# In the last 256 tokens the copy-out waits for the skip score, and the whole order is planned anew

## The chip, the cores and the metric

The kernel runs on one core of a Trainium2 chip. The metric is the time of one execution in microseconds (us) as the device measures it, as the median of several runs. TensorE (PE) does the matrix products, VectorE (DVE), ScalarE (ACT) and GpSimd (POOL) the elementwise work, and SyncE (SP) issues nearly all transfers.

## The reference, cut to what matters

Three stages follow each other for 4 x 768 = 3072 tokens of 8 heads x 48 = 384 channels: a linear attention with a complex decay, a wide elementwise layer between two matrix products, and a gated mixture of experts that runs only for tokens whose skip score is above zero.

```
S = a_t * S + k_t v_t^T          # complex decay a_t, the real part is read
y_t = q_t S                      # 3072 tokens x 384
h = y @ w_in                     # 384 x 2048
g = (a0 + a1 h + a2 h^2 + a3 h^3) / (1 + |b0||h| + |b1| h^2 + 1e-6)
x = g @ w_out                    # 2048 x 384
skip = x @ w_skip                # one score for each token
out = x, and for tokens with skip > 0 an expert's output is added
```

With the inputs of this case the flags that the kernel works out at its end (is any token's score positive, is any decay out of range) are zero, and the branch to the experts isn't taken: the profile ends with the flags and the closing of the program.

## The kernel before, in words

**Units, chunks and steps.** The tokens are worked in 12 units of 256 tokens (u = 0 to 11), each of two chunks of 128. For a chunk the attention part makes decay sums (`cumx`, `cuml`: matmuls L651 to L681), rotated keys and queries, their transposes (`xp`, L729, onto PE and evicted by `xpe`, L735 on ACT or L737 on DVE), scores (`sc`, L749), their mask (`msk`, L754 on DVE), outputs (`ymm`, L772 and L774), the update of the state (`upd`, L795), and the output's eviction (`yev`, L813 or L814), a transfer inside SBUF (`ysd`) and its rounding (`xhi`, L827). Products L749, L772, L774 and L795 use PE in column tiles of 64 ("column-tiled" below); all others use the whole array.

For a unit the wide layer has 8 steps (p = 0 to 7). A step has two halves of G1 (L886, into a `zb` bank, 9 matmuls each), the elementwise chain (ACT L866 and L387, DVE L870), the split of its result in a rounded part `gh` (L915) and a remainder `gl` (L918), and two G2 (L938, 6 matmuls each, accumulated over the 8 steps into `ob[0]` and `ob[1]`, one for each half of the tokens). Unit 0 does G1 and G2 with unsplit float32 weights, because splitting the weights (`whi` L480, `wlo` L485) is done while it runs; later units use a three-product split.

**At the end of a unit** `ob[t]` is copied with a scale into `x2` (`ev`: L387 on ACT or L951 on DVE), sent to the output (`st`), and read once more by DVE for the skip score (`sk`, L956). The first G2 of the next unit may write `ob[t]` when both have read it. Before, `sk` names `x2` among what it reads, so it always follows the copy.

**What sets the order.** A planner, `Plan.order`, runs on the host: it has a cost for each task, a latency for each hop, ranks with an offset for each kind of task and unit (the table `PP`), and picks for each engine the next task. The result is written out as a fixed order for each engine; there is no choice left on the chip. Where the planner sees PE without work ahead of `start(NP) + X1`, `filled` puts dummy matmuls there (L1025, L1029 and, after the first 48, L1032): they keep PE running, and since they stand in PE's order, they take their time on the chip whether PE is idle or not.

**The end of the program.** After the last `sk`, `flags` (L1329 to L1338) sums the flags, PE adds them over the partitions (L1335), and all engines load the result, branch, and close.

Of the kernel before, what the change touches and what calls it, by code (L numbers as in the profile page):

```python
# [29 lines left out]
class Plan:  # L30
# [36 lines left out]
    def order(self, slack, bias, ahead, hold, cold, only):  # L67
# [22 lines left out]
        def finish(t, end, e):  # L90
            for s in t.succ:
                wait[s.n] -= 1
                lat = self.LAT[e] if e else 0.0
                if len(s.opts) == 1 and s.opts[0][0] == e and e != "SP":
                    lat = 0.06
                ready_at[s.n] = max(ready_at[s.n], end + lat)
                if wait[s.n] == 0:
                    if s.only and s.only[0].eng != s.only[1]:
                        done[s.n] = True
                        finish(s, ready_at[s.n], None)  # L100
                    else:
                        heapq.heappush(events, (release(s), 1, s.n, None))
# [78 lines left out]
    def filled(self, out, first, last, gap, each, fn):  # L181
# [6 lines left out]
                end = max(end, at + cost)  # L188
            fns.append((at, len(fns), f))
        return [f for _, _, f in sorted(fns, key=lambda x: x[:2])]  # L190
PP = dict(RK={('e1', 3): -0.0, ('qr', 1): 6.96, ('d3', 3): 13.1, ('sk', 3): -33.76, ('msk', 1): -5.9, ('e6', 3): -0.19, ('cumx', 1): -2.3, ('xhi', 2): 6.15, ('e5', 3): 0.49, ('G2', 1): -4.22, ('a5', 2): 2.01, ('a2', 1): -8.56, ('dec', 1): -3.76, ('kr', 1): -14.26, ('lda', 0): 5.23, ('e4', 3): 21.04, ('ev', 3): -14.56, ('prr2', 2): 5.78, ('consts2', 0): -4.33, ('tlo', 3): -1.17, ('e8', 2): 8.49, ('ev', 0): -21.56, ('consts', 0): -6.3, ('a5', 3): 1.52, ('upd', 1): 11.25, ('e7f', 2): -15.18, ('prr1', 1): -3.2, ('G1', 2): -3.49, ('xlo', 2): -3.85, ('ldk', 2): 15.32, ('G2', 2): 13.59, ('d4', 1): -1.28, ('xp', 2): -0.57, ('S2', 2): -13.35, ('alo', 2): 6.39, ('e7f', 3): 4.78, ('yev', 1): -13.54, ('prr1', 3): 0.46, ('tlo', 2): 16.11, ('dec', 3): 8.54, ('e9', 3): 4.88, ('ysd', 1): -1.18, ('e1', 1): -4.49, ('last', 3): -1.04, ('cry', 3): 0.22, ('a2', 0): 5.36, ('S2', 1): 7.88, ('xabs', 0): 14.95, ('upd', 3): 1.28, ('cadd', 1): -16.46, ('e11', 2): -3.49, ('qr', 3): -3.75, ('ldq', 0): 31.15, ('a4', 2): 2.25, ('red', 2): -8.46, ('rnd', 2): 3.88, ('lnexp', 0): -3.85, ('wldi', 0): 0.65, ('e9', 2): 19.04, ('G1', 3): -3.79, ('e2', 1): 2.32, ('lda', 1): 6.73, ('ldv', 1): 2.97, ('exq', 1): 2.55, ('thi', 3): -1.29, ('a2', 3): 1.22, ('kr', 2): 11.48, ('a4', 0): -4.77, ('e2', 3): -0.12, ('S', 1): 1.63, ('ev', 1): 40.5, ('e6', 1): -7.3, ('d1', 3): -1.59, ('e11', 1): 1.23, ('rnd', 3): 25.29, ('e3', 1): 3.94, ('sc', 2): 4.01, ('e9', 1): -5.69, ('a4', 1): -1.23, ('e13', 0): 20.66, ('last', 0): 4.52, ('sc', 1): -6.19, ('cry', 1): -8.01, ('wb3', 0): -0.35, ('clear', 0): -0.5, ('upd', 0): -1.87, ('ysd', 2): -2.76, ('e4', 1): -2.8, ('st', 1): -33.79, ('e3', 2): 9.5, ('kr', 3): 1.89, ('gl', 2): -3.18, ('xpe', 2): 1.47, ('e8', 1): 0.91, ('e7', 3): -0.07, ('xp', 3): -0.38, ('cuml', 2): 8.38, ('a5', 0): -0.18, ('sk', 1): -8.68, ('e8', 3): -2.46, ('sk', 0): 0.63, ('ldk', 3): 0.52, ('xabs', 3): 3.07, ('e11', 3): 7.67, ('a1', 2): -0.63, ('xhi', 0): 19.42, ('prr2', 3): 0.27, ('d2', 3): -4.57, ('wb2', 0): 0.47, ('S', 0): 5.86, ('e1', 2): 28.44, ('rnd', 1): 5.16, ('last', 1): -9.33, ('prr1', 0): 18.07, ('e7', 2): -0.5, ('yev', 3): -1.48, ('e8', 0): 0.22, ('msk', 2): -4.38, ('exq', 2): -4.69, ('ldc', 0): 8.32, ('st', 3): -5.42, ('ysd', 0): -16.93, ('exp', 2): 14.54, ('qr', 0): 7.46, ('upd', 2): 0.53, ('S2', 0): 22.86, ('trig', 0): -0.15, ('lda', 2): -11.3, ('st', 2): -4.62, ('cf', 0): -11.69, ('xlo', 1): 0.91, ('xp', 0): 1.47, ('cuml', 0): 0.35, ('xp', 1): 0.1, ('e10', 1): 10.75, ('e2', 2): 1.32, ('ldv', 3): -1.82, ('exp', 0): 1.38, ('d1', 2): 0.8, ('last', 2): -3.81, ('cuml', 1): 4.83, ('e10', 2): 18.95, ('ysd', 3): 5.28, ('xlo', 3): 1.57, ('ymm', 1): -2.42, ('exp', 3): 5.64, ('exq', 0): 4.26, ('whi', 0): 0.0, ('gl', 3): 1.62, ('exp', 1): 0.28, ('dec', 2): -0.18, ('ldv', 2): 0.29, ('e5', 1): -0.67, ('e5', 0): -0.28, ('qr', 2): -5.24, ('red', 1): 0.08, ('ahi', 2): -0.51, ('e6', 2): -11.75, ('gh', 3): -0.5, ('exq', 3): 2.27, ('xpe', 0): -1.55, ('cumx', 2): -2.59, ('st', 0): 13.52, ('e6', 0): 5.22, ('cry', 2): -0.66, ('ymm', 0): 1.91, ('S', 3): 0.34, ('e7f', 1): 3.39, ('ldk', 0): 1.33, ('e3', 0): -8.95, ('xhi', 1): 5.57, ('sk', 2): 3.32, ('G2', 3): -0.73, ('d4', 3): 1.65, ('ldq', 2): 12.25}, FU=1, C2=5.371, C3=117.794, AF=1.733, P0=3.406, P1=8.248, NO={'whi': ('POOL',), 'prr2': ('POOL',), 'prr1': ('POOL',), 'gh': ('ACT', 'DVE'), 'cadd': ('DVE',), 'wlo': ('DVE',), 'tlo': ('DVE',)}, E0=8.284, E1=-3.522, TC=16, WS=(0, 1, 2, 3, 4, 5, 0, 1, 1, 0, 1, 2, 2, 1, 2, 2), HO={('tlo', 'POOL'): 0.482, ('tlo', 'DVE'): 0.437, ('gl', 'POOL'): 0.129, ('cadd', 'DVE'): 0.404, ('xpe', 'DVE'): 0.549, ('prr1', 'DVE'): 0.413, ('last', 'POOL'): 0.369, ('ev', 'DVE'): 0.055, ('xabs', 'DVE'): 0.192, ('xhi', 'DVE'): 0.444, ('prr1', 'POOL'): 0.11, ('xlo', 'DVE'): 0.101, ('whi', 'ACT'): 0.177, ('gh', 'DVE'): 0.558, ('prr2', 'POOL'): 0.087, ('gh', 'ACT'): 0.067, ('last', 'ACT'): 0.097}, DW=54.14194888235853, WL=7, P=6.353, LAG2=4.235, SL={'ACT': 2.875, 'DVE': 0.975, 'POOL': 0.839, 'SP': 0.306, 'PE': 1.002, '2': 2.13}, X1=34.585, T0=55.875, NZ=6, NH=3, CU=2, BI={'DVE': 67.612, 'POOL': -2.285})


def main_part(tc, ctx, q, k, v, a_re, a_im, w_in, w_out, moe_a, moe_b, w_skip, out, keep):
# [661 lines left out]
    def step(s):  # L856
# [88 lines left out]
        if p == NP - 1:  # L945
            for t in range(2):
                o, x = ob[t][:, 0:DM], x2[t]
                ti = 2 * u + t
                X2 = ("x2", t)
                pl.add([act(0.47, x, o, AF.Copy, scale=fine["sg"]),  # L950
                        ("DVE", 0.53, lambda x=x, o=o: nc.vector.tensor_scalar(  # L951
                            out=x, in0=o, scalar1=fine["sg"], scalar2=None, op0=ALU.mult))],
                       reads=[("o", t), "cf"], writes=[X2], name="ev", due=at(1, 3))
                pl.add(dma((out[ti * 128:(ti + 1) * 128, :], x)), reads=[X2], writes=[("out", ti)], name="st", due=at(1, 5))
                sk_ = ("zk", ti)
                pl.add([("DVE", 0.65, lambda o=o, ti=ti, sk_=sk_: nc.vector.scalar_tensor_tensor(  # L956
                    out=zb[pl.slot[sk_]][:, 0:DM], in0=o, scalar=fine["sg"], in1=wsk, op0=ALU.mult, op1=ALU.mult,
                    accum_out=skip[:, ti:ti + 1]))],
                       reads=["wsk", "cf", ("o", t), X2], bank=sk_, free=sk_, name="sk", due=at(1, 3))
# [477 lines left out]
```

## Time and profile before

| | |
|---|---|
| time, median of 3 runs | 647.55 us (646.91 to 648.62) |
| the profiled execution's own time | 647.43 us |
| its span, first to last instruction | 645.7 us |
| PE busy | 633.9 us, 98% of the span |
| DVE busy, ACT busy, POOL busy | 558.0, 558.7, 332.2 us |
| dummy matmuls L1032 in the profile | 270 records, two for each of 135 instructions |

The sum in the prediction is made against the profiled execution: 1.7 us of its 647.43 lie outside the span. A matmul's end in the profile is modelled, so matmuls overlap in the rows; the distance from one start to the next tells what one costs.

### The profile page before, as it was taken

The numbers are of one execution on the slowest core, as the hardware profiler recorded it, in microseconds if no ns is written. First come the engines' busy times: TensorE is split into PE (matmuls) and PEld (weight loads), VectorE is DVE, ScalarE is ACT, GpSimd is POOL, SyncE is SP. The second block draws the span as 40 slices with busy tenths as digits, with TensorE's granted clock in tenths as the row PEclk, the third lists the DMA queues.
The fourth block names the chain that finished last, engine by engine and source line by source line (L and its number), as shares of the span: only waits on it lengthen the run. The fifth ranks groups of instructions, "written<-read, shape, count | busy, mean of one in ns | idle before, by whom it ended". The sixth has DMA issues, their size and how long they took to land.

```text
span 645.7 us, 14813 instructions
## 1 busy us (share of the span) xinstructions
PE 633.9 (98%) x5720; PEld 590.3 (91%) x5720; DVE 558.0 (86%) x901; ACT 558.7 (87%) x925; POOL 332.2 (51%) x349
## 2 busy tenths in 40 slices
PE   9999999999999999999999999999999999999994
PEld 8888887789999989999999999999999999989994
DVE  6999999898889987897988989998978997876873
ACT  5889989997899997897999998997998997976771
POOL 5145269397636447547367366545557554522221
PEclk9999999999999999999999999999999999999998
DMA  8955114010401303103112203103112200000000
GB/s 316 401 187 169 50 35 157 16 34 21 123 3 44 99 26 115 39 14 115 30 44 59 78 14 91 52 29 97 53 37 67 68 17 23 19 29 5 19 6 32
DMA packets 29777, 45.79 MB, mean 71 GB/s; under 512 B 5760, under 2 KB 23552, under 8 KB 29696
## 3 DMA queue, kind: packets, MB, share of 16 engines
q1 hardware_dynamic: 29408, 44.73, 21.3%
q8 instruction: 47, 0.77, 0.5%
q14 instruction: 34, 0.28, 0.2%
q10 hardware_dynamic: 288, 0.00, 0.0%
HBM read 38.73 MB, written 4.72 MB: 67 GB/s over the span
## 4 chain that ended last, share of the span: by engine, by line
PE 81%; ACT 12%; DVE 4%; issue 2%; POOL 0%; DVEq 0%; ACTq 0%; POOLq 0%
PE zb L886 27%; PE ob L938 25%; PE zb L729 6%; PE zb L749 5%; PE ob L1032 4%; PE zb L772 4%; PE zb L795 3%; PE zb L774 3%; ACT wk L387 2%; ACT wk L866 2%; ACT tb L548 1%; DVE wk L870 1%; PE zb L678 1%; ACT L584 1%; ACT zb L866 1%
## 5 line engine op out<-in xcount | busy, mean ns | idle before, releaser
L870 DVE SCALAR_TENSOR_TENSOR wk<-wk,cf,zb 128x512 f32<-128x512 f32 x192 | 141.7, 742 | 33.0 <-ACT zb L866 26.3
L886 PE MATMUL zb<-xh,wi 128*128 128x256 f32 x528 | 152.4, 289 | 0.0
L886 PE MATMUL zb<-xl,wi 128*128 128x256 f32 x528 | 147.9, 280 | 0.0
L886 PE MATMUL zb<-xh,li 128*128 128x256 f32 x528 | 147.8, 280 | 0.0
L387 ACT ACTIVATE wk<-wk,cf 128x512 f32<-128x512 f32 x192 | 139.8, 732 | 1.4
L915 POOL TENSOR_SCALAR gh<-wk 128x512 fp32r<-128x512 f32 x88 | 61.4, 698 | 147.3 <-PE ob L938 69.4
L938 PE MATMUL ob<-wo,gh 128*128 128x384 f32 x352 | 120.4, 342 | 0.8 <-DVE zb L956 0.8
L938 PE MATMUL ob<-wo,gl 128*128 128x384 f32 x352 | 118.6, 337 | 0.0
L938 PE MATMUL ob<-lo,gh 128*128 128x384 f32 x352 | 118.2, 336 | 0.0
L918 POOL TENSOR_TENSOR gl<-wk,gh 128x512 fp32r<-128x512 f32 x69 | 99.2, 1438 | 5.3
L886 PEld LDWEIGHTS zb<-xh,wi 128*128 128x128 f32 x528 | 99.5, 188 | 2.7 <-issue 1.0
L886 PEld LDWEIGHTS zb<-xl,wi 128*128 128x128 f32 x528 | 99.7, 189 | 0.6
L886 PEld LDWEIGHTS zb<-xh,li 128*128 128x128 f32 x528 | 99.4, 188 | 0.0
L866 ACT ACTIVATE wk<-zb 128x512 f32<-128x512 f32 x96 | 57.4, 598 | 31.1 <-PE zb L886 30.6
L870 DVE SCALAR_TENSOR_TENSOR zb<-wk,cf,zb 128x512 f32<-128x512 f32 x96 | 71.7, 748 | 0.0
L938 PEld LDWEIGHTS ob<-wo,gh 128*128 128x128 f32 x352 | 66.1, 188 | 2.7 <-issue 2.4
L870 DVE SCALAR_TENSOR_TENSOR wk<-wk,zb 128x512 f32<-128x512 f32 x96 | 65.5, 683 | 1.6
L866 ACT ACTIVATE wk<-zb,cf 128x512 f32<-128x512 f32 x96 | 66.4, 691 | 0.1
L938 PEld LDWEIGHTS ob<-wo,gl 128*128 128x128 f32 x352 | 66.1, 188 | 0.1
L938 PEld LDWEIGHTS ob<-lo,gh 128*128 128x128 f32 x352 | 66.2, 188 | 0.0
L866 ACT ACTIVATE zb<-wk 128x512 f32<-128x512 f32 x96 | 58.2, 608 | 7.7 <-DVE wk L870 7.0
L749 PEld LDWEIGHTS zb<-qT,kT 112*64 112x64 f32 x768 | 35.4, 137 | 5.9 <-ACT qT L735 3.1
(166 smaller groups left out, 1326.9 us busy)
## 6 DMA issues: line engine op xcount, KB each, us to landing
vb<-in_v_dram SPq DMA_DIRECT2D x24, 288.0 KB, 3.0
ws<-in_moe_w_in_dram SPq DMA_DIRECT2D x8, 768.0 KB
ws<-in_moe_w_out_dram SPq DMA_DIRECT2D x8, 768.0 KB, 8.9
kraw<-in_k_dram SPq DMA_DIRECT2D x12, 384.0 KB, 3.8
qraw<-in_q_dram SPq DMA_DIRECT2D x12, 384.0 KB, 3.8
out_dram<-x2b SPq DMA_DIRECT2D x24, 192.0 KB, 1.9
ar<-in_a_re_dram SPq DMA_DIRECT2D x11, 384.0 KB
ai<-in_a_im_dram SPq DMA_DIRECT2D x11, 384.0 KB, 5.7
```

The costliest lines, as they stand in the source:

```text
L387: return ("ACT", cost, lambda: nc.scalar.activation(out=out, in_=in_, func=func, **kw))
L729: nc.tensor.transpose(z[0:112, i, :], src[:, 112 * h:112 * h + 112], ident)
L749: nc.tensor.matmul(z[o:o + 64, h, n:128], lhsT=K[:, h, n:n + 64], rhs=Q[:, h, n:128], start=True, stop=True)
L772: nc.tensor.matmul(dst, lhsT=vt, rhs=pT[hf][:, i, :], start=True, stop=first)
L774: nc.tensor.matmul(dst, lhsT=state[:, 48 * h:48 * h + 64], rhs=qT[hf][:, i, :], start=False, stop=True)
L866: return ("ACT", cost, lambda: nc.scalar.activation(out=h() if out is None else out, in_=h() if in_ is None else in_, func=func, **kw))
L870: return ("DVE", cost, lambda: nc.vector.scalar_tensor_tensor(out=h() if out is None else out, in0=in0, scalar=scalar, in1=h(), op0=op0, o ...
L886: nc.tensor.matmul(h()[:, i * 256:i * 256 + 256], lhsT=w[:, 128 * j:128 * j + 128], rhs=x[:, j, :], start=(n == 0), stop=(n == 3 * len(pr) ...
L915: nc.gpsimd.tensor_scalar(out=g, in0=uu, scalar1=1.0, scalar2=1.0, op0=ALU.mult, op1=ALU.mult)
L918: eng[e].tensor_tensor(out=ghl("gl", s), in0=uu, in1=ghl("gh", s).bitcast(F32), op=ALU.subtract)
L938: nc.tensor.matmul(o, lhsT=a[:, sl], rhs=w, start=(f == 0 and n == 0), stop=(f == NF - 1 and n == len(pr) - 1))
L1032: nc.tensor.matmul(ob[0][:, 384:512], lhsT=ident, rhs=ident, start=n == 32, stop=True, skip_group_check=True)
```

## The change

In the last unit `sk` no longer reads `x2` but `ob[t]` alone, and `ev` follows `sk`. The rounding of the weights (`whi`) gets a third option, on DVE. The planner's latency between two tasks of one engine goes from 0.06 to 0.12 us, and the table `PP` (some 200 numbers, of which a line would tell nothing) is another one; it bars `whi` from DVE and POOL (`NO={'whi': ('DVE', 'POOL'), ...`), and moves the dummies' window and the due times.

```
                 if len(s.opts) == 1 and s.opts[0][0] == e and e != "SP":
-                    lat = 0.06
+                    lat = 0.12
...
+            elif e == "DVE":
+                nc.vector.tensor_scalar(out=hi, in0=weight_f(m, p), scalar1=1.0, scalar2=None, op0=ALU.mult)
...
-        pl.add([("ACT", 0.73, lambda: whi("ACT")), ("POOL", 0.85, lambda: whi("POOL"))], ...
+        pl.add([("ACT", 0.73, lambda: whi("ACT")), ("POOL", 0.85, lambda: whi("POOL")), ("DVE", 0.47, lambda: whi("DVE"), True)], ...
...
-                       reads=[("o", t), "cf"], writes=[X2], name="ev", due=at(1, 3))
+                           reads=[("o", t), "cf"] + ([("sk", t)] if u == NU - 1 else []), writes=[X2], name="ev", due=at(1, 3))
...
-                       reads=["wsk", "cf", ("o", t), X2], bank=sk_, free=sk_, name="sk", due=at(1, 3))
+                           reads=["wsk", "cf", ("o", t)] + ([] if u == NU - 1 else [X2]), writes=[("sk", t)], bank=sk_, free=sk_, name="sk", due=at(1, 3))
...
+                for f in (score, evict) if u == NU - 1 else (evict, score):
+                    f()
```

**In the built program.** Nearly every row on every engine stands elsewhere. The work on PE is the same matmuls, but for the dummies L1032 (L1040 after the change): 135 before, 129 now. Between full-array work, PE's order has 78 runs of column-tiled matmuls before and 84 now. `whi` is 16 instructions on ACT in both, and none on DVE. Of the tasks with a choice of engine, 8 `xpe` move from DVE to ACT (96 on ACT now), 13 `gl` from POOL to DVE (32 now), 6 `xlo`, 4 `qr` and 5 of the scalings L465 to POOL, 6 `cadd` from POOL to DVE.

Three places are shown. The first is PE's order in the program's first tenth, from the state update of the second chunk (L795, L797 after) or the decay sums (L681, L683 after) to the first G1 of unit 0 (L886, L888 after, on `fi`, the unsplit weights). Before:

```order
L795 MATMUL zb_83<-vb_96,kt_107 64x48 x16
L1032 MATMUL ob_77<-ident 128x128 x2
L681 MATMUL zb_79<-ta_154,trir 128x384
L681 MATMUL zb_82<-ta_154,trir 128x384
L1032 MATMUL ob_77<-ident 128x128 x6
L654 MATMUL zb_83<-ai_142,trit 128x384
L1032 MATMUL ob_77<-ident 128x128 x7
L886 MATMUL zb_83<-xh_4_614,fi_297 128x256 x6
```

And now:

```order
L776 MATMUL zb_79<-qT_109,state 64x128 x2
L683 MATMUL zb_82<-ta_153,trir 128x384
L683 MATMUL zb_84<-ta_153,trir 128x384
L797 MATMUL zb_79<-vb_96,kt_107 64x48 x16
L1040 MATMUL ob_77<-ident 128x128 x11
L888 MATMUL zb_81<-xh_4_620,fi_300 128x256 x3
L656 MATMUL zb_79<-ai_142,trit 128x384
```

Between the second chunk's outputs and the first G1 stand 11 dummies in place of 15, and the sum L654 (L656 now) has moved behind the first matmuls of G1.

The second place is PE at the end of unit 5. `ob_77` and `ob_78` are the two accumulators; nine matmuls of G1 stand just ahead of these rows and, ahead of them, the last G2 of unit 5 on `ob_77`. Before:

```order
L938 MATMUL ob_78<-wo_1387,gh_1404 128x384
L938 MATMUL ob_78<-lo_1547,gh_1404 128x384
L938 MATMUL ob_78<-wo_1387,gl_1442 128x384
L938 MATMUL ob_78<-wo_1387,gh_1404 128x384
L938 MATMUL ob_78<-lo_1547,gh_1404 128x384
L938 MATMUL ob_78<-wo_1387,gl_1442 128x384
L938 MATMUL ob_77<-wo_1060,gh_1404 128x384
```

And now, with three groups of transposes between the nine of G1 and the first row:

```order
L940 MATMUL ob_78<-wo_1423,gh_1378 128x384
L940 MATMUL ob_78<-lo_1562,gh_1378 128x384
L940 MATMUL ob_78<-wo_1423,gl_1427 128x384
L940 MATMUL ob_78<-wo_1423,gh_1378 128x384
L940 MATMUL ob_78<-lo_1562,gh_1378 128x384
L940 MATMUL ob_78<-wo_1423,gl_1427 128x384
L731 MATMUL zb_82<-ident,qt_105 112x128 x4
L751 MATMUL zb_83<-qT_108,kT_110 64x128 x2
L751 MATMUL zb_83<-qT_108,kT_110 64x64 x2
L751 MATMUL zb_83<-qT_108,kT_110 64x128 x2
L751 MATMUL zb_83<-qT_108,kT_110 64x64 x2
L940 MATMUL ob_77<-wo_1079,gh_1378 128x384
```

The first G2 of unit 6 on `ob_77` has moved back behind four groups of transposes and one of scores.

The third place is the end of ACT's and DVE's order. The order is the same, and what the rows wait for is not (in brackets, the semaphores of the engines). ACT before, with the copies L387 of `ob` and the load of the flags:

```order
L387 ACTIVATE wk<-wk,cf 128x512 [waits Activation_49] x2
L866 ACTIVATE zb_81<-wk 128x512 [waits DVE_49,Activation_49]
L387 ACTIVATE x2b<-ob_77,cf 128x384 [waits DMAHW4_49,PE_49]
L387 ACTIVATE x2b<-ob_78,cf 128x384 [waits DMAHW5_49,PE_49]
L1364 TENSOR_LOAD fazi [waits DVE_49]
```

And DVE now, with the scores L961 (L956 before), whose waits were for `Activation_49`:

```order
L920 TENSOR_TENSOR gl_1427<-wk,gh_1378 128x512 [waits PE_49,Pool_49]
L961 SCALAR_TENSOR_TENSOR zb_84,skip<-ob_77,cf,wsk 128x384 [waits PE_49]
L961 SCALAR_TENSOR_TENSOR zb_81,skip<-ob_78,cf,wsk 128x384 [waits PE_49]
L1337 TENSOR_SCALAR fat_7024,fam<-skip 128x24 [waits DVE_49]
L1345 CAST fazi<-faz 1x2 [waits PE_49]
```

The scores now wait for PE alone, and ACT's two copies wait for DVE in place of PE.

## Rows read from the trace of the kernel before

**Rows 1.** The page: busy time, share of the span and instructions of each engine.
```profile
PE 633.9 (98%) x5720; PEld 590.3 (91%) x5720; DVE 558.0 (86%) x901; ACT 558.7 (87%) x925; POOL 332.2 (51%) x349
```

**Rows 2.** Busy time of each engine by stretch: us, PE, PEld, DVE, ACT, POOL, PEclk.
```profile
20.00:40.00 20.00, 19.97 (x213) 18.17 (x212) 19.87 (x38) 17.10 (x26) 7.06 (x7) 1.00 0.91 337
340.00:360.00 20.00, 20.00 (x160) 19.62 (x157) 17.75 (x28) 17.75 (x33) 13.67 (x14) 1.00 0.29 82
```

**Rows 3.** Chain of waits at the start (start, us, what), and the dummies' group.
```profile
21.30 1.36 PE zb L681 x4
22.66 5.36 PE ob L1032 x48
L1032 PE MATMUL ob<-ident 128*128 128x128 f32 x270 | 33.0, 276 | 0.0
```

**Rows 4.** Chain of waits: G1 and G2 undisturbed, G1 after L795, scores after either.
```profile
167.00 1.06 PE zb L886 x9
168.06 2.08 PE ob L938 x12
...
363.50 1.27 PE zb L886 x9
...
426.46 1.49 PE zb L749 x32
...
435.41 1.35 PE zb L749 x32
```

**Rows 5.** PE's waits: for whom, total us, times, longest.
```profile
PE ob L938 <- DVE zb L956: 0.8, 2, 0.5
PE zb L886 <- ACT xh L827: 0.3, 1, 0.3
```

**Rows 6.** Timeline of PE and DVE at the end of unit 5.
```profile
370.70 0.34 PE L938 MATMUL ob<-wo,gl 128*128 128x384 f32 x1
371.27 0.41 PE L938 MATMUL ob<-wo,gh 128*128 128x384 f32 x1 [0.23 <-DVE zb L956]
...
370.44 0.62 DVE L956 SCALAR_TENSOR_TENSOR zb<-ob,cf,wsk 128x384 f32<-128x384 f32 x1
370.98 0.14 DVE L956 DVE_READ_ACCUMULATOR zb<-ob,cf,wsk 128x1 f32 x1
```

**Rows 7.** Timeline of PE at a wait for an eviction.
```profile
329.26 0.34 PE L938 MATMUL ob<-wo,gl 128*128 128x384 f32 x1
329.76 0.65 PE L729 MATMUL zb<-ident,qt 128*112 128x128 f32 x4 [0.16 <-ACT kT L735]
```

**Rows 8.** Chain at the start, then ACT's timeline there.
```profile
48.48 0.92 PE zb L795 x32
...
55.20 2.86 PE zb L886 x12
...
48.58 0.60 ACT L813 ACTIVATE ys<-zb 128x512 f32<-128x512 f32 x1
...
53.02 0.84 ACT L480 ACTIVATE wi<-fi 128x768 fp32r<-128x768 f32 x1
53.77 0.56 ACT L664 ACTIVATE cs<-zb,magic 128x384 f32<-128x384 f32 x1
...
54.65 0.51 ACT L827 ACTIVATE xh<-ys 128x384 f32<-128x384 f32 x1
```

**Rows 9.** Timeline of the program's end.
```profile
636.51 0.34 PE L938 MATMUL ob<-wo,gl 128*128 128x384 f32 x1
636.89 0.58 ACT L387 ACTIVATE x2b<-ob,cf 128x384 f32<-128x384 f32 x1 [0.46 <-PE ob L938]
...
637.51 0.63 DVE L956 SCALAR_TENSOR_TENSOR zb<-ob,cf,wsk 128x384 f32<-128x384 f32 x1 [0.36 <-ACT x2b L387]
```

**Rows 10.** DVE's group for one weight operation; the copy-out's transfer to landing (us).
```profile
L458 DVE TENSOR_SCALAR zb<-ws 128x384 int32<-128x384 int32 x32 | 17.1, 554 | 0.1
out_dram<-x2b SPq DMA_DIRECT2D x24, 192.0 KB, 1.9
```

More of the change, by code (lines that the diff above doesn't have):

```diff
@@ L485, in wlo @@
             eng[e].tensor_tensor(out=weight_lo(m, p), in0=weight_f(m, p), in1=weight_hi(m, p).bitcast(F32), op=ALU.subtract)
-        pl.add([("ACT", 0.73, lambda: whi("ACT")), ("POOL", 0.85, lambda: whi("POOL"))], reads=w, writes=h_ + [("st", (p + (NP if m == "o" else 0)) // 2)], name="whi")
+        pl.add([("ACT", 0.73, lambda: whi("ACT")), ("POOL", 0.85, lambda: whi("POOL")), ("DVE", 0.47, lambda: whi("DVE"), True)], reads=w, writes=h_ + [("st", (p + (NP if m == "o" else 0)) // 2)], name="whi")
         pl.add([("POOL", 1.85, lambda: wlo("POOL")), ("DVE", 0.87, lambda: wlo("DVE"), True)],
@@ L949, in step, with evict, score @@
                 X2 = ("x2", t)
-                pl.add([act(0.47, x, o, AF.Copy, scale=fine["sg"]),
-                        ("DVE", 0.53, lambda x=x, o=o: nc.vector.tensor_scalar(
-                            out=x, in0=o, scalar1=fine["sg"], scalar2=None, op0=ALU.mult))],
-                       reads=[("o", t), "cf"], writes=[X2], name="ev", due=at(1, 3))
[L954 to L958, printed above, removed]
-                       reads=["wsk", "cf", ("o", t), X2], bank=sk_, free=sk_, name="sk", due=at(1, 3))
+                def evict(o=o, x=x, ti=ti, X2=X2, t=t):
+                    pl.add([act(0.47, x, o, AF.Copy, scale=fine["sg"]),
+                            ("DVE", 0.53, lambda x=x, o=o: nc.vector.tensor_scalar(
+                                out=x, in0=o, scalar1=fine["sg"], scalar2=None, op0=ALU.mult))],
+                           reads=[("o", t), "cf"] + ([("sk", t)] if u == NU - 1 else []), writes=[X2], name="ev", due=at(1, 3))
+                    pl.add(dma((out[ti * 128:(ti + 1) * 128, :], x)), reads=[X2], writes=[("out", ti)], name="st", due=at(1, 5))
+                def score(o=o, ti=ti, X2=X2, t=t):
+                    sk_ = ("zk", ti)
+                    pl.add([("DVE", 0.65, lambda o=o, ti=ti, sk_=sk_: nc.vector.scalar_tensor_tensor(
+                        out=zb[pl.slot[sk_]][:, 0:DM], in0=o, scalar=fine["sg"], in1=wsk, op0=ALU.mult, op1=ALU.mult,
+                        accum_out=skip[:, ti:ti + 1]))],
+                           reads=["wsk", "cf", ("o", t)] + ([] if u == NU - 1 else [X2]), writes=[("sk", t)], bank=sk_, free=sk_, name="sk", due=at(1, 3))
+                for f in (score, evict) if u == NU - 1 else (evict, score):
+                    f()
     NC = NT // 128
```

2 lines of the change are left out of this document (1 added, 1 removed).

## The prediction

> **What bounds the kernel now.** I read the page first. PE is busy in 98% of the span, DVE and ACT in 86 and 87% [rows 1]: the end of PE's work, and the short tail behind it, set the time. The page alone can mislead here, since PE's share contains the dummies. They are 270 records of L1032, and 48 of them in a row take 5.36 us, so 0.112 us a record and 0.223 us for an instruction of two [rows 3]; 135 instructions are 30 us, all in the first tenth of the program.
>
> Next the busy time by stretch: from 20 to 40 us DVE is the full engine (19.87 of 20 us), while PE looks full because of the dummies; from 340 to 360 PE is full with real work and DVE and ACT have 2.2 us to spare in 20 [rows 2]. The granted clock is 1.00, the higher level of 2.4 GHz, in both stretches; I see no cost of the clock in the sum.
>
> So the time is PE's list of work, plus what PE loses, plus the tail. A busy PE hides small losses, because modelled ends overlap. I therefore looked at starts: G1's nine matmuls take 1.06 us undisturbed, twelve of G2 2.08 us, so 0.118 and 0.173 us from start to start [rows 4]. Where a start comes later and the instruction has a wait, that is a loss. I found eleven such places between 55 and 476 us, of 0.15 to 0.71 us, 3.3 us together. PE's own waits show only a part of it: 0.8 us in two waits for the skip score, 0.3 us for the rounded attention output [rows 5]. One of the two shows the pattern: G2 starts at 370.70 and the next one, into the other accumulator, at 371.27 in place of 370.87, because DVE read that accumulator for the score until 371.12 [rows 6]: 0.39 us lost by the regular pitch (0.57 less 0.17 to 0.18). Another: a transpose starts at 329.76, where the G2 matmul ahead of it started at 329.26, because it waits for ACT's eviction [rows 7]: some 0.33 us.
>
> **The change part by part.** *The weights' rounding on DVE.* The built order has it 16 times on ACT and never on DVE, as before: the new option costs and gives nothing. What it would relieve, ACT at the start, keeps its load.
>
> *The tail.* Before: the last matmul starts at 636.51, ACT copies from 636.89 for 0.58 us, DVE scores from 637.51, and the flags follow it [rows 9]. Now DVE scores where ACT began, at about 636.89, and all behind it moves up by 637.51 - 636.89 = 0.62 us. What is late next is the copy: it starts at about 637.6 (0.63 of the score and a hop of 0.03 to 0.1), ends by 638.2, and its transfer, 1.9 us from issue to landing in the middle [rows 10], lands by some 640.5. The span ends at 645.7, so it is covered as long as the closing behind the flags stays longer than that; SP issues it at about 638.2 for a third of a us and comes to the flags' load at about 638.5, when the flags are ready too. I take -0.62; bounds 0 (SP or the landing sets the end) and -0.65.
>
> *The dummies.* Six fewer: -6 x 0.223 = -1.34 us [rows 3]. This counts in full only if the work behind is ready; where it isn't, PE waits instead, which I count among the losses.
>
> *Runs of column-tiled work.* 84 in place of 78. G1 right behind one takes 1.27 us in place of 1.06: 0.21 us to leave [rows 4]. Two blocks of scores take 1.49 us behind full-array work and 1.35 behind other column-tiled work: 0.14 to enter. So 0.35 a run, 6 x 0.35 = +2.1 us. Beside transposes I found the way out dearer and the way in cheaper; the new runs stand partly among them and among dummies, so the bounds are 1.6 and 2.8. The Trainium skill, page "TensorEngine Tiling (Array Packing)", section "Key Properties", says that a change of the tiling mode drains TensorE, which speaks against this change; the 0.35 us agrees in kind. By that rule alone each added run costs something and the sum of this part would be positive; it gives no size, so the sum goes by the rows.
>
> *Losses that go.* At the end of each unit PE must not come back to `ob[t]` before copy and score are done. In PE's list I summed the work that stands between the last G2 of a unit and the first of the next on the same accumulator, by the pitches above. Before: 2.11 us in four of the 22 places; two of these are the two waits. Now one has 2.11 (end of unit 1), all others 3.1 to 12.8. Likewise from a unit's transposes to its first scores: before, 10 places have under 1.5 us; now two, both in the first 85 us. From scores to the masked product 12 places had under 2 us, now four. So nearly all the 3.3 us should go: -3.3 with bounds 0 and -3.3.
>
> *Losses that come.* At the start the first G1 needs the rounded output of the second chunk. Before, from the start of the state update behind that chunk's product (48.48) to G1 (55.20) are 6.7 us, the last 0.49 of them lost; ACT evicts at 48.58 and is done with the rounding at 55.16 [rows 8]. Now PE has, in between, two decay sums (1.36 us [rows 3]), the update (0.92), 11 dummies (2.45): 4.7 us. ACT has two operations less in that stretch, a rounding of weights (0.75 us from its start at 53.02 to the next) and a rounding of phases (about 0.44, as two operations fill 53.77 to 54.65 [rows 8]), so its 6.6 us become some 5.4: 0.7 us lost. The one place with 2.11 us at an accumulator may lose 0.4 again, and the two or three short returns at the start 0.4. Together +1.5, with bounds 0.3 and 4: what a table with other offsets does at places that I didn't sum can't be read from before.
>
> *Moved between engines.* DVE gets 13 remainders and 6 carries and gives off 8 evictions, 6 remainders of the attention output and 4 products; ACT gets the evictions and gives off 5 scalings. By their rows' durations that is within 5 us for each over 646, where both have some 90 us idle: nothing on the path, except by queueing at the start, which is in the bound of 4.
>
> **The sum.** -0.62 - 1.34 + 2.1 - 3.3 + 1.5 = -1.7 us, from 647.43 to 645.7 us for an execution (span 644.0). The median before, 647.55, lies 0.1 above the profiled execution, so that is -0.3% against it. About 0.3%, 1.9 us, is what a measurement of this kernel can tell from no change: the forecast stands just inside.
>
> **The rivals.** *All waits go.* If the new table leaves only 0.3 us of losses: -0.62 - 1.34 + 2.1 - 3.0 = -2.9, 644.5 us; with the cheaper column runs 644.0. For it: every distance that I summed grew, at accumulators by a factor of 1.5 to 6. Against: the start, where DVE has no slack and G1 is asked for earlier.
>
> *Losses only change place.* The eleven go and as many others come, 3 to 4 us at places with other partners (queueing on ACT, which now does all evictions of transposes): -0.62 - 1.34 + 2.1 + 0 to 1 = +0.1 to +1.1, 647.5 to 648.6 us. For it: before, the order was planned in the same way and still lost 3.3 us, and the wait of rows 7 is behind ACT's queue, not behind a short distance alone.
>
> *The start runs dry, slower.* PE's place in the list asks for unit 0's weights and attention before DVE delivers them. One block of weights is six DVE operations of 0.55 us [rows 10], some 2.8 us at their pitch; two blocks ordered ahead of what PE waits for would cost 5.6 us. DVE has only 0.13 us idle from 20 to 40 us [rows 2], so nothing takes that back. -0.62 - 1.34 + 2.1 - 3.3 + 0.8 + 5.6 = +3.2, 650.6 us. It decides from some 4.3 us of such waits on. Against it: I summed DVE's work ahead of PE's places in both orders, and until 125 us DVE stands as far ahead now as before, within 1 us at the tightest places.
>
> *The tail gives nothing*, since the closing hangs on something else: 646.3 us, inside the forecast's own range.
>
> **How the numbers follow.** Forecast (losses between 0.6 and 2.6 us, time 644.8 to 646.8): 0.55. All waits go, 644.0 to 644.8: 0.17. Losses only change place, 646.8 to 649.4: 0.18. Slower start, 649.5 to 651: 0.10. The range 644.2 to 649.2 leaves out the slow rival and a piece of the fast one. Faster by over 0.3% (under 645.6): all of the second case and four tenths of the first, 0.39. Slower (over 649.5): 0.10. Within: 0.51.
>
> **What would show it.** In the new profile: (1) the score starts within 0.1 us of the last matmul's modelled end and the stretch from that matmul to the end is 0.6 us shorter; (2) 258 records of L1040; (3) G1 behind column-tiled work still 1.27, and 84 such runs; (4) PE's waits for the score at the ends of units gone, at most one left; (5) the first G1 waits for the rounded output, some 0.7 us, at about 54. The prediction is wrong if PE's first 125 us show waits of over 2 us, if later starts behind waits sum to over 3 us, or if PE's own pitch differs between the two.

## The result, and the profile after

The changed kernel takes 655.32 us (median, 654.56 to 655.53), the kernel before in the same comparison 648.01 (646.91 to 648.87): ratio 1.0111, 95% interval 1.0098 to 1.0124, some 7.3 us slower. The forecast was 645.7 with a range of 644.2 to 649.2, so it was wrong, in sign too. The profiled execution has a span of 653.9 us, 8.2 more than before.

First the lines of the page, TensorE's waits and the dummies' group after the change, which answer to [rows 1], [rows 5] and [rows 3].

```profile
PE 636.7 (97%) x5708; PEld 592.1 (91%) x5708; DVE 562.7 (86%) x901; ACT 555.4 (85%) x923; POOL 321.6 (49%) x345
```
```profile
PE zb L731 <- DVE kt L390: 4.2, 1, 4.2
...
PE faz L1343 <- ACT x2b L387: 1.4, 1, 1.4
```
```profile
L1040 PE MATMUL ob<-ident 128*128 128x128 f32 x258 | 34.0, 284 | 0.0
```

The waits for the skip score are gone, as forecast, and one long wait is new, of 4.2 us (beside two of 0.6 and 0.3): the transposes L731 of unit 2's first rotated key wait for DVE. The busy times by stretch around it (us, PE, PEld, DVE, ACT, POOL, granted clock, then transfers):

```profile
120.00:122.00 2.00, 2.00 (x19) 2.00 (x18) 1.93 (x4) 1.99 (x3) 1.92 (x3) 1.00 0.00 0
122.00:124.00 2.00, 0.29 (x3) 0.10 (x1) 1.93 (x3) 1.04 (x2) 1.92 (x2) 1.00 0.00 0
124.00:126.00 2.00, 0.00 (x0) 0.00 (x0) 2.00 (x2) 0.00 (x0) 1.57 (x1) 0.91 0.00 0
126.00:128.00 2.00, 1.49 (x7) 1.49 (x8) 2.00 (x4) 0.35 (x1) 0.00 (x0) 0.50 0.00 0
...
130.00:132.00 2.00, 2.00 (x11) 2.00 (x11) 0.67 (x1) 1.17 (x3) 0.00 (x0) 0.50 0.00 0
132.00:134.00 2.00, 2.00 (x22) 1.53 (x21) 0.55 (x2) 1.82 (x4) 0.00 (x0) 0.89 0.00 0
```

PE stands idle from 122.3 to 126.5. Within that wait the granted clock falls (0.91 in the stretch from 124 to 126), and it is 0.50, the lower level of 1.2 GHz, until about 132.5: the transposes and the dummies among them run at half speed. DVE is full all the while. What it does there, with its timeline and then GpSimd's (start, duration, engine):

```profile
118.37 0.65 DVE L344 TENSOR_SCALAR cf<-cf 128x2 int32<-128x2 int32 x1
119.05 0.48 DVE L365 TENSOR_SCALAR rsum<-cf 128x2 f32<-128x2 f32 x1
119.56 0.46 DVE L344 TENSOR_SCALAR cf<-cf 128x2 int32<-128x2 int32 x1
120.06 1.76 DVE L367 TENSOR_TENSOR cf<-cf 128x1 f32<-128x1 f32 x1
121.75 0.14 DVE L344 TENSOR_SCALAR cf<-cf 128x1 int32<-128x1 int32 x1
121.92 1.79 DVE L369 TENSOR_SCALAR cf<-cf 128x2 f32<-128x2 f32 x1
123.75 0.17 DVE L370 RECIPROCAL cf<-cf 128x2 f32<-128x2 f32 x1
123.95 1.64 DVE L371 TENSOR_TENSOR rsum<-cf 128x2 f32<-128x2 f32 x1
125.51 0.94 DVE L390 TENSOR_TENSOR kt<-r,cs 128x768 f32<-128x768 f32 x1
```
```profile
119.97 1.84 POOL L487 TENSOR_TENSOR li<-fi,wi 128x768 fp32r<-128x768 f32 x1
121.89 1.80 POOL L487 TENSOR_TENSOR lo<-fo,wo 128x768 fp32r<-128x768 f32 x1
123.77 1.80 POOL L487 TENSOR_TENSOR li<-fi,wi 128x768 fp32r<-128x768 f32 x1
```

Eight operations on one or two columns take 7.2 us (118.37 to 125.59). The long ones end where a weight remainder on GpSimd ends: 121.82 and 121.81, 123.71 and 123.69, 125.59 and 125.57. Before, the same eight stood at 75.63 to 77.05, 0.15 to 0.17 us each, in a gap of GpSimd's:

```profile
76.48 0.17 DVE L369 TENSOR_SCALAR cf<-cf 128x2 f32<-128x2 f32 x1
```
```profile
77.71 0.57 POOL L610 TENSOR_SCALAR cs<-cs 1x384 f32<-1x384 f32 x1 [5.96 <-DMA cs<-xr]
```

They are one task of the planner, the last part of `coefs2`, whose results only the flags need. Its price there is 1.3 us, plus once the rest of what GpSimd is doing; in the new order it was put at 119.48 for 1.98 us. The prediction did not look at it.

The program's end after the change, which answers to [rows 9]:

```profile
643.12 0.34 PE L940 MATMUL ob<-wo,gl 128*128 128x384 f32 x1
643.50 0.63 DVE L961 SCALAR_TENSOR_TENSOR zb<-ob,cf,wsk 128x384 f32<-128x384 f32 x1 [0.38 <-PE ob L940]
644.22 0.18 DVE L1337 TENSOR_SCALAR_CACHE_REDUCE fat<-skip 128x24 f32<-128x24 f32 x1
644.22 0.58 ACT L387 ACTIVATE x2b<-ob,cf 128x384 f32<-128x384 f32 x1 [0.48 <-DVE zb L961]
644.85 0.19 PE L1343 MATMUL faz<-fam,one 128*1 128x2 f32 x2 [1.39 <-ACT x2b L387]
645.08 0.15 DVE L1345 CAST fazi<-faz 1x2 int32<-1x2 f32 x1 [0.67 <-PE faz L1343]
```

The last matmul starts at 643.12, 6.6 us later than before [rows 9]. The other 1.6 us of the span lie at its very end: TensorE's last semaphore comes 1.64 us behind SyncE's, before 0.01 behind it; VectorE's last comes with SyncE's in either kernel. The table, from the records of the semaphores, has it for all kernels of this study. "List" is the time from the first decay sum of TensorE's list (L654, L656 after) to the last matmul; that sum starts at 14.9 to 16.2 us, from one execution to the next (13.6 and 14.3 in the two kernels with fewer dummies ahead of it).

| kernel | TensorE records | list, us | last matmul at | SyncE's last semaphore behind it | TensorE's |
|---|---|---|---|---|---|
| before | 5720 | 620.88 | 636.51 | 9.13 | 9.14 |
| after | 5708 | 627.39 | 643.12 | 9.13 | 10.77 |
| e1_cf_late | 5708 | 620.14 | 635.60 | 9.02 | 10.58 |
| e2_dry_recip | 5708 | 620.42 | 636.13 | 9.09 | 11.16 |
| e3_filled | 5746 | 624.96 | 639.86 | 9.02 | 9.03 |
| e4_before_cf_busy | 5720 | 628.87 | 644.04 | 9.04 | 9.05 |
| e5_fewer_dummies | 5680 | 619.84 | 636.02 | 9.41 | 9.42 |
| e6_flag_bank | 5708 | 620.20 | 635.51 | 9.09 | 10.58 |
| e7_tail_undone | 5708 | 620.79 | 636.57 | 9.02 | 10.51 |
| e8_dry_forms | 5708 | 624.88 | 639.93 | 9.22 | 10.72 |
| e9_early_dummies | 5696 | 620.77 | 634.37 | 9.61 | 9.62 |
| e10_less_at_61 | 5668 | 619.89 | 635.30 | 9.46 | 9.48 |
| e11_trimmed | 5656 | 621.63 | 635.96 | 9.21 | 9.22 |
| e12_same_count | 5708 | 620.16 | 636.18 | 9.15 | 10.44 |

Each row of the table is one execution. Four kernels that differ little in what they do up to the last matmul (e1, e2, e6, e7) have lists from 620.14 to 620.79, so a difference under 0.65 us between two rows tells nothing. One of the twelve executions of e12_same_count ran at a mean clock of 0.751 and took 779.96 us; its time and ratio below are those of the other eleven.

The rows of DMA queue q8, which the page calls "instruction", tell more of the closing. Where TensorE's last semaphore is late, it stands 1.34 to 1.62 us behind the end of that queue's last packet of 16 KB (after the change 10.77 and 9.24 us behind the last matmul, in e1 10.57 and 9.10). Where it isn't late, it keeps no such distance (-0.30 to +1.12). At the branch, in all fourteen kernels, TensorE's first record stands 1.35 to 1.62 us behind the end of a packet of 16 KB. So a late closing fits a wait of TensorE for its own last instructions; that it is one, no run shows.

### The profile page after: what moved, and what is told of

It is laid out like the page before. It is cut to its first block, busy times and chain, and to the rows that moved or that the text cites. A ratio compares the mean times of both kernels' runs of the same rounds, so it can differ in the third digit from the quotient of the medians.

```text
span 653.9 us, 14722 instructions
## 1 busy us (share of the span) xinstructions
PE 636.7 (97%) x5708; PEld 592.1 (91%) x5708; DVE 562.7 (86%) x901; ACT 555.4 (85%) x923; POOL 321.6 (49%) x345
## 4 chain that ended last, share of the span: by engine, by line
PE 84%; DVE 7%; ACT 6%; issue 1%; DMA 0%; POOL 0%; SPq 0%; ACTq 0%; DVEq 0%; POOLq 0%
PE ob L940 28%; PE zb L888 28%; PE zb L731 6%; PE zb L751 5%; PE zb L774 4%; PE ob L1040 3%; PE zb L797 3%; PE zb L776 2%; DVE wk L872 1%; DVE zb L458 1%; PE ob L1033 1%; DVE zb L461 1%; ACT tb L550 1%; DVE ai L553 1%; ACT wk L868 1%
## 5 line engine op out<-in xcount | busy, mean ns | idle before, releaser
L888 PE MATMUL zb<-xh,wi 128*128 128x256 f32 x528 | 152.3, 288 | 0.0
L888 PE MATMUL zb<-xl,wi 128*128 128x256 f32 x528 | 148.0, 280 | 0.0
L888 PE MATMUL zb<-xh,li 128*128 128x256 f32 x528 | 147.9, 280 | 0.0
L387 ACT ACTIVATE wk<-wk,cf 128x512 f32<-128x512 f32 x192 | 140.5, 735 | 0.8
L888 PEld LDWEIGHTS zb<-xh,wi 128*128 128x128 f32 x528 | 99.4, 188 | 3.5 <-issue 2.7
L888 PEld LDWEIGHTS zb<-xl,wi 128*128 128x128 f32 x528 | 99.6, 189 | 0.0
L888 PEld LDWEIGHTS zb<-xh,li 128*128 128x128 f32 x528 | 99.4, 188 | 0.0
L920 POOL TENSOR_TENSOR gl<-wk,gh 128x512 fp32r<-128x512 f32 x56 | 80.9, 1445 | 4.3
```

The source lines that it names most:

```text
L387: return ("ACT", cost, lambda: nc.scalar.activation(out=out, in_=in_, func=func, **kw))
L888: nc.tensor.matmul(h()[:, i * 256:i * 256 + 256], lhsT=w[:, 128 * j:128 * j + 128], rhs=x[:, j, :], start=(n == 0), stop=(n == 3 * len(pr) ...
L920: eng[e].tensor_tensor(out=ghl("gl", s), in0=uu, in1=ghl("gh", s).bitcast(F32), op=ALU.subtract)
```

## The experiments

Theory A: the eight small operations wait for GpSimd, the key is late, PE waits, and the clock's fall doubles the damage. Rival B: the order asks for the key too early in any case. Rival C: the clock falls there for a reason of its own.

**e1_cf_late: the eight operations elsewhere.** `out_` is the planned order, its first field the planned time; the eight, planned at 390, run at 389.32 to 390.75 us in e1's trace, 0.15 to 0.17 us each.

```
+    out_ = [(390.0,) + x[1:] if x[3] == "cf" and x[0] > 100 else x for x in out_]
```

> The changed kernel with nothing else altered than the place of eight small coefficient operations of VectorE (L344, L365, L367, L369 to L371, 128x2 and smaller): they leave the place ahead of unit 2's first rotated key, where each lay beside GpSimd's weight remainders and the eight took 7.2 us (118.37 to 125.59), and are issued at about 397 us, where GpSimd and VectorE are idle. Theory A (the small operations wait for GpSimd's running instruction, the key comes late, TensorE waits 4.2 us and then works at the lower clock until 133): the wait and the clock's fall both go, 7.1 us less than the changed kernel, 647.5 to 649 us, mean clock 0.997. Rival B (the order asks for the key too early anyway, and the eight count only with their undisturbed 1.3 us): 2.9 us of wait remain and the clock still falls, 652.5 to 654 us. Rival C (the clock falls there for a reason of its own): only the 4.2 us go, 651 us, mean clock 0.99.

Measured: 647.88 us, ratio to before 1.000 (0.999 to 1.001), mean clock 0.996. The 4.2 us are gone from PE's waits, and the stretch has the full clock:

```profile
120.00:130.00 10.00, 10.00 (x104) 8.65 (x103) 9.04 (x13) 9.99 (x18) 8.18 (x6) 1.00 0.01 2
```

Moving these eight operations takes back 7.4 us, as much as the whole difference between the changed kernel and the kernel before. B and C fall. The closing is still late in e1 (10.58 in the table), and the ratio of 1.000 includes that.

**e2_dry_recip: other small operations in their place.**

```
+    def dry():
+        a, b = cf[:, 14:16], cf[:, 16:18]
+        for i in range(8):
+            nc.vector.reciprocal(out=(a, b)[i % 2], in_=(b, a)[i % 2] if i else cf[:, 10:12])
```

> As the run with the small operations moved to about 397 us, but eight other small operations stand in their old place: reciprocals of 128x2 on scratch columns, each waiting for the one before, one SBUF input each. Theory A in its narrow form (what waits for GpSimd are operations with two SBUF inputs and the elementwise tensor_scalar of 128x2, not a reciprocal; the one reciprocal among the eight took 0.17 us right beside a GpSimd instruction): eight times 0.17 to 0.2 us, 1.4 to 1.6 us together, the key is there in time, 647.5 to 649 us, clock 0.997. Rival D (any small operation there is slow, by the hops between them or by GpSimd's being busy at all): 6 to 7 us for the eight, TensorE waits again some 4 us, 654.5 to 656 us.

Measured: 647.58 us, ratio 0.9994 (0.9984 to 1.0004). The eight take 1.55 us, beside GpSimd's L487 and L465:

```profile
118.32 1.55 DVE L1029 RECIPROCAL cf<-cf 128x2 f32<-128x2 f32 x8
```

So neither their number nor the hops between them are slow; the form of operation is.

**e8_dry_forms: which forms wait.** In the same place six `tensor_scalar` of one column, then four of two columns.

> As the run with eight reciprocals in the old place of the small operations, but with six tensor_scalar operations of 128x1 and then four of 128x2 there, each on scratch columns and each waiting for the one before. Theory A in its form by operation (the 128x2 tensor_scalar waits for GpSimd's running instruction, as at 118.37, 119.05, 119.56 and 121.92 in the changed kernel; 128x1 is not known, since the only one there fell between two GpSimd instructions): the four of 128x2 take 0.4 to 1.8 us each while GpSimd works. If size alone decides (an even number of columns), the six of 128x1 take 0.14 to 0.2 us each beside a running GpSimd instruction; rival: they wait as well, 0.4 us and more each.

Measured (one execution: 652.25 us). DVE's groups, mean ns of one at the row's end:

```profile
L1031 DVE TENSOR_SCALAR cf<-cf 128x2 f32<-128x2 f32 x4 | 4.2, 1038 | 0.1
L1031 DVE TENSOR_SCALAR cf<-cf 128x1 f32<-128x1 f32 x6 | 0.9, 153 | 0.2
```

One column is never held, though five of the six run beside a GpSimd instruction from end to end. Of the four of two columns three are held, up to 1.77 us, each to within 0.03 us of the end of a GpSimd instruction, and one gets in between two of these in 0.17. The four alone made PE wait 2.3 us, and the clock fell behind that wait too (0.55 and 0.60 from 124 to 128). The Trainium skill, page "Advanced Engine Details and Errata", section "Mode Summary", says that GpSimd and VectorE's modes with two ports block each other, and that such a mode wants operands in SBUF with sizes both even, or both odd and above one, and equal; its section "GPSIMD Details" adds operations with two SBUF inputs (L367 and L371 here). The trace agrees, with 1.04 us on the mean against 0.15.

**e3_filled: the key as late, PE kept busy.** 19 dummies more ahead of the transposes that wait.

```
+    hold_ = next(x for x in out_ if x[3] == "xp" and x[0] > 120)
+    out_[out_.index(hold_)] = hold_[:2] + (lambda f=hold_[2]: ([idle() for _ in range(19)], f()),) + hold_[3:]
```

> The changed kernel with 19 more dummy instructions (38 records, 4.2 us at 0.223 us each) on TensorE right ahead of the transposes that wait for the late key; the eight small operations stay where they are. The key is as late as before. Theory A (the clock falls because TensorE stands idle 4.2 us): the clock stays at 1.00, the transposes start at about 126.5 as before, and what ran at half speed from 126.5 to 133.3 runs at full speed: 2.9 us less than the changed kernel, 652 to 653 us, mean clock 0.997. Rival C (the clock falls for another reason, such as what the other engines draw or the kind of work behind): clock 0.99 again, 655 to 656 us.

Measured: 651.29 us, a little under the range, ratio to before 1.0058 (1.0042 to 1.0074), and the clock stays:

```profile
124.00:126.00 2.00, 2.00 (x19) 1.83 (x18) 2.00 (x3) 0.00 (x0) 0.75 (x1) 1.00 0.00 0
126.00:128.00 2.00, 2.00 (x21) 2.00 (x19) 2.00 (x4) 1.63 (x4) 0.00 (x0) 1.00 0.00 0
```

Useless matmuls in the gap make the kernel faster by 4.0 us by the medians: 2.4 in TensorE's list (627.39 to 624.96), and the rest as much as its closing, which isn't late here (9.03 in place of 10.77); the range had not reckoned with that. So it is the idle time that brings the clock down, at 2.4 us, and the wait itself costs some 4.8 (624.96 to 620.14).

**e4_before_cf_busy: the damage done to the kernel before.** There, too, only the planned time of that task is changed, to 106.

> The kernel before with nothing altered but the place of the same eight small operations: they leave their place at 75.6 to 77.1, where GpSimd is idle and the eight took 1.4 us, and are issued at about 105.8, where GpSimd runs weight remainders back to back from 102.2 to 114.3. Theory A: about one of the eight gets in between two GpSimd instructions of 1.8 us, so the eight take 7 to 9 us, VectorE comes 6 to 8 us late to work that has some 1.6 us of slack until 125, and TensorE waits 4 to 6 us; with the clock falling behind that wait 4 to 10 us more than the kernel before, 652 to 658 us. Rival B (eight small operations count 1.3 us wherever they stand): 647.5 to 649.5 us.

Measured: 655.2 us, ratio 1.0114 (1.0099 to 1.0128). The eight take 6.6 us (105.41 to 111.99), a little under the range, because only four are held (0.93 to 1.66 us each), where six are in the changed kernel. PE's wait and two of DVE's rows:

```profile
PE ob L938 <- DVE wk L870: 5.0, 1, 5.0
```
```profile
106.58 1.66 DVE L344 TENSOR_SCALAR cf<-cf 128x2 int32<-128x2 int32 x1
108.27 0.16 DVE L367 TENSOR_TENSOR cf<-cf 128x1 f32<-128x1 f32 x1
```

This one task, moved by 30 us, gives the old order as large a loss as the new one has.

**e7_tail_undone and e6_flag_bank: the tail.** Both are e1 with one thing more. In e7 the last unit's copy stands ahead of the score again; in e6 five unused PSUM tiles stand ahead of the flags' one.

> The run with the small operations moved, and the last unit's order taken back (copy, then score, as in the kernel before). Theory T3 (the edit brings the flags' cast forward by 0.3, and the longer load of the flags beside the output's transfer takes that back): cast at 2.27 us behind the last matmul, loads of the flags 0.47 to 0.55 us, semaphores' clearing at 8.6 to 8.7 us behind the last matmul, the same as with the edit (8.60). Rival T4 (the prediction: all behind the score moves by 0.62): clearing at 9.2.

> The run with the small operations moved, and the small PSUM tile of the closing's flags placed five banks further on, away from the two accumulators. In the changed kernel the flags' matmul (L1343) starts 1.73 us behind the last matmul, though VectorE has been ready since 1.28: it waits for ScalarE's last copy. Theory T1 (it waits since its tile lies in an accumulator's bank, which that copy still reads): the matmul starts at about 1.3, the flags' cast at 1.5 in place of 1.96 us behind the last matmul. Rival T2 (it waits for all readers of the released pool, whichever bank it takes): cast at 1.96 as now.

Measured, in us behind the last matmul: e7 score 0.99, cast 2.27, loads of the flags 2.63 to 3.12, clearing of the semaphores 8.61; e1 0.38, 1.96, 2.32 to 3.10, 8.60; e6 0.38, 1.96, 2.32 to 3.11, 8.68. T3 holds. The score is 0.61 earlier, as forecast; half of that goes to the flags' matmul, which now waits for the copy, wherever its tile lies (T1 falls; it fits T2), and the other half to the load, which ends 3.1 us behind the last matmul in either order. What holds the load is in no row.

**e5_fewer_dummies, e10_less_at_61, e9_early_dummies: what a dummy costs.** e5 is e1 with the dummies' window closed at 110 in place of 134.5 planned; e10 is e5 without six dummies at 61 us; e9 is e1 without six at the start (`range(32, 38)` in the second piece).

```
-    fns = pl.filled(out_, 5.0, start(NP) + PP["X1"], 0.3, 0.22, idle)
+    fns = pl.filled(out_, 5.0, 110.0, 0.3, 0.22, idle)
```
```
         n = len(begun)
         begun.append(1)
+        if n in range(126, 132):
+            return
```

> The run with the eight small operations moved to about 397 us, and the last 14 dummy instructions taken out (those planned behind 110 us: 5 at 113.7, 9 between 121.2 and 124.2 in that run's trace). If each dummy counts in full, as the prediction took it, 14 times 0.223 = 3.1 us less, 644.5 to 645 us. By the readiness of what stands behind them (remainder of the attention output ready at 114.23 where TensorE took it up at 114.92; first rotated key ready at 120.00, taken up at 121.85; the evictions between the transposes ready 0.05 us before they are used) some 0.7 us at the first place and 0.7 to 1 us at the second: 1.2 to 1.8 us less, 646.0 to 646.7 us. Rival (VectorE holds everything up there, the dummies only fill): no gain, 647.5 to 648.2 us. The clock stays at 1.00 in all three, since no gap is over 1 us.

> The run with the last 14 dummies taken out, and six of the 17 dummies fewer that stand from 61.2 to 65.0 us, ahead of a matmul that was ready 3.66 us before it started. Counted in full: the last matmul 1.34 us earlier than in that run (636.02), at 634.7, and 645.3 us. If VectorE sets the pace there: within 0.4 us of 636.0, and 646.2 to 647.0 us.

> The run with the small operations moved, and six dummies fewer at the program's start, in the group that ends at 15.46 in that run's trace, where what stands behind has been ready since 13.51; TensorE has 12 records less. Two questions. First, the price of six dummies where VectorE is the full engine behind them: if each counts in full as in the prediction, the last matmul starts 1.34 us earlier than in that run (635.60), at 634.3; if VectorE sets the pace of the first 120 us, it comes within 0.4 us of 635.6, since TensorE only waits longer later. Second, the closing: in the changed kernel and in five runs with just as many TensorE instructions TensorE's last semaphore comes 1.4 to 2.1 us behind those of the other engines, in the three with other counts and in the kernel before with them. Theory L (it hangs on the length of TensorE's program): with 12 records less it comes with them, and the time is 1 to 1.6 us under the kernel before's plus 0.1, 646.2 to 647 us. Rival M (it hangs on something else in the changed order): late again by 1.4 to 2.1 us, 647.5 to 648 us.

Measured: e5 646.67 us, ratio 0.9984 (0.9975 to 0.9993); e10 646.89, 0.9982 (0.9973 to 0.9991); e9 646.13, 0.9971 (0.9960 to 0.9982). Fourteen late dummies, 3.1 us, shorten the list by 0.3 (620.14 to 619.84), less than the spread, where 1.2 to 1.8 had been expected, and six at 61 us do nothing (619.89): PE waits in their place, in e5 up to 2.0 us at once, where no wait over 1 had been expected. That e5's time lies in its range all the same is luck: its closing isn't late (9.42 in place of e1's 10.58), and nor is that of e10 and e9.

For the six at the start, the dummies ahead of the first decay sum, first in e1, then in e9:

```profile
12.33 3.29 PE L1041 MATMUL ob<-ident 128*128 128x128 f32 x28
15.46 0.81 PE L656 MATMUL zb<-ai,trit 128*128 128x384 f32 x2
```
```profile
11.81 1.95 PE L1043 MATMUL ob<-ident 128*128 128x128 f32 x16
13.60 0.91 PE L656 MATMUL zb<-ai,trit 128*128 128x384 f32 x2
```

The sum comes 1.86 us earlier and the last matmul 1.23, but 0.52 of either is that this group began earlier in this one execution. From the group's start to the last matmul it is 623.27 us in e1 and 622.56 in e9: 0.71 are left, about half of the full 1.34 and hardly more than the spread. e9 is the fastest kernel here, 0.29% under the kernel before; e1's ratio is 1.000, so e9 is some 1.9 us under e1 too. Half of that is the closing: with 5696 records TensorE's last semaphore is not late, 1.0 us under e1's (theory L).

**e11_trimmed: all trims together.**

> The small operations moved to about 397 us, and all three trims of dummies together: six at the start, six at 61 us, and the last 14; 26 instructions, 52 records fewer. If the three add up as they did one by one (last matmul 1.23, 0.72 and 0.3 us earlier), the last matmul starts at about 633.4 and, if TensorE's closing comes with the others, the time is 644.9 to 645.7 us, 0.4% under the kernel before. If they take each other's room, since VectorE has to be waited for once: 645.7 to 646.5 us.

Measured: 647.14 us, above the ranges of both theories, ratio 0.9981 (0.9971 to 0.9992): they don't add up. PE's longest wait has the same 2.0 us as in e5, but the clock falls behind it. First e5's, then e11's stretches:

```profile
120.00:124.00 4.00, 2.00 (x18) 1.76 (x16) 3.05 (x4) 3.97 (x7) 3.92 (x3) 1.00 0.00 0
124.00:128.00 4.00, 3.91 (x34) 2.79 (x36) 4.00 (x6) 4.00 (x8) 3.92 (x2) 1.00 0.01 4
```
```profile
120.00:124.00 4.00, 1.97 (x10) 1.97 (x11) 3.09 (x4) 3.90 (x8) 3.84 (x3) 0.76 0.00 0
124.00:128.00 4.00, 4.00 (x38) 2.78 (x37) 3.02 (x6) 3.66 (x7) 2.03 (x1) 0.82 0.00 0
```

Of e11's twelve executions the five with a mean clock of 0.995 to 0.997 took 645.38 to 646.33 us, the seven with 0.992 to 0.994 took 647.04 to 648.41. The late dummies buy no work. In the traces, the clock stays up through this stretch in e1, with them, and falls in e11, without them; but it stays in e5 too, which lacks them as well. What decides between e5 and e11 no run shows.

**e12_same_count: the closing.** e9, with six matmuls of one column in place of the six dummies.

> The run with six dummies fewer at the start, with six matmuls of one column in their place, so that TensorE has as many records as the changed kernel (5708) again, at less of their time. Theory L (TensorE's late last semaphore hangs on the length of its program): late again by 1.4 to 2.1 us behind the other engines', last matmul at 634.3 to 635.1, 647 to 648 us. Rival M (the six early dummies themselves made the difference, by where the time of the rest falls): not late, 645.9 to 646.8 us.

Measured: 647.42 us, ratio 0.9991 (0.9983 to 1.0000). TensorE's last semaphore is late again, by 1.3 us, but the last matmul came at 636.18, not at 634.3 to 635.1. The six matmuls did not take less of TensorE's time:

```profile
12.89 1.39 PE L1034 MATMUL ob<-ident 128*128 128x1 f32 x12
14.15 2.03 PE L1044 MATMUL ob<-ident 128*128 128x128 f32 x16
16.01 0.81 PE L656 MATMUL zb<-ai,trit 128*128 128x384 f32 x2
```

Their twelve records take 1.26 us from start to start, 0.105 each; a dummy of 128 columns takes 0.112 (28 in 3.13 us in e1). So this kernel gave back the time together with the count, and alone it does not part L from M. The table speaks for L: the seven kernels with 5708 records all have the late closing, by 1.3 to 2.1, with lists from 620.14 to 627.39, and the seven with other counts don't, with lists from 619.84 to 628.87. That the count itself is what acts, and not the place at which TensorE's last instructions come to lie in its program, no run shows; the packets of q8 under the table fit either.

## Why the prediction was wrong, step by step

**The step that failed** is "losses that come" at the start, and the argument against the rival of a start that runs dry: "until 125 us DVE stands as far ahead now as before, within 1 us at the tightest places". That sum took each operation of DVE by its own row, so the eight small ones as 1.4 us (75.63 to 77.05). They took 7.2, because of what GpSimd ran beside them: 5.8 us more on an engine without slack, and a wait of 4.2 for PE. The rival had the right place, but priced another cause, and 0.10 was far too little for it. e1, e2, e4 and e8 show this cause: in e2 eight other operations of two columns in the same place take 1.55 us, and PE doesn't wait.

**The clock** is the second: "I see no cost of the clock in the sum" was read from stages in which PE never stood still. A wait on PE was counted at its length; e3 shows that this one cost half as much again: 4.8 us of the list for the wait, 2.4 for the clock.

**The tail** was mis-sized: -0.62 forecast, 0.0 measured (clearing at 8.71 behind the last matmul, before 8.72). The bound of 0 was in the text, with SP or the landing as its reason; it was the copy and the load.

**The closing** was taken as the same. It is 1.6 us longer in the changed kernel's trace; that goes with the number of TensorE's records, which no step of the forecast looked at.

**The dummies** (-1.34) counted all alike. e5 and e10 show that those behind 110 us and those at 61 are worth less than the spread, because PE waits in their place, and e9 leaves about half for six at the start. The prediction also put all 135 of the kernel before in the first tenth; seven of them stand at 105 us. By place the new order has 94 up to 60 us, 21 from 61 to 106 and 14 behind 113, the old one 104, 31 and none. Whether the 1.34 came can't be read from any run.

**What held.** Without tail, closing and the late key, the forecast was -1.34 + 2.1 - 3.3 + 1.5 = -1.04 us. In the four kernels in which the new order has the key in time and all its dummies (e1, e2, e6, e7), the list is 0.74, 0.46, 0.68 and 0.09 us shorter than before. These are single executions with a spread of 0.65, so they don't speak against the forecast and don't bear it out; its terms +1.5 (losses that come) and +2.1 are parted from the others by no run. The 258 records are there; G1 behind column-tiled work takes 1.25 and 1.26 us (at 248.78 and 274.87, 1.27 before [rows 4]); none of PE's waits is for the score. Most of the 3.3 us of late starts did go: in e1's trace two are left from 125 us on, some 0.3 us at 226.3 and 0.4 at 227.3. The loss of 0.7 us at the first G1 did not come: in e1's trace that matmul starts at 52.75, 0.15 behind ACT's rounding, which ends at 52.60. The whole new order, without its late key but with its late closing, is worth nothing that can be measured against the old one (ratio 1.000).

## What to carry to other kernels

A VectorE operation is priced by what GpSimd runs beside it, not by its size: before summing a full engine's work from its rows, look for operations with two SBUF inputs, or a `tensor_scalar` of even width in SBUF, that land beside long GpSimd instructions, however small they are. (Large ones are held too: L553 on 128x768 takes 2.40 us at 111.26 beside GpSimd after the change, and 0.95 at 115.50 before; e1 has the same 2.40, and there PE doesn't wait for it.) A chain of them pays GpSimd's instruction again and again, so work that nobody waits for belongs where GpSimd is idle. And a wait on TensorE costs more than its length when the clock falls behind it, so dummies in a gap can pay for themselves even where they cover nothing.

## What had not been expected of the hardware

- A `tensor_scalar` of 128x2 is held to the end of GpSimd's instruction (three of four in e8, 1.04 us on the mean of the four), one of 128x1 is not (0.15 us), nor is a reciprocal of 128x2 (eight in 1.55 us).
- The granted clock fell within waits of TensorE of 4.2 and 5.0 us, behind one of 2.3, and behind one of 2.0 in e11 but not behind one of 2.0 in e5.
- A matmul of one column takes 0.105 us of TensorE's time here, a dummy of 128 columns 0.112.
- TensorE's closing comes 1.3 to 2.1 us late in the seven kernels with 5708 TensorE records and in none of the seven with another count (5656 to 5746). The late ones stand 1.34 to 1.62 us behind the last 16 KB packet of DMA queue q8; that TensorE waits for its instructions there is likely and not shown.
